# Slot sums over 32 features at a time, with VectorE's 32x32 turns in place of TensorE's transposes

## The chip, the cores and the metric

The kernel runs on one core of a Trainium2 chip. The metric is the device time of one execution in microseconds (us); three runs are given, and their median counts. One profiled execution gives the trace. Engines: PE is the matrix engine (PEld its weight loads), DVE is VectorE, ACT is ScalarE, POOL is GpSimd, SP issues most DMAs.

## What is computed

Attention with 32 memory slots for each of 8 batch entries and 8 heads (576 tokens, 64 features a head), then a mixture of 8 experts on the 4608 tokens. Cut to what matters:

```python
a = softmax(phi)                           # over 32 slots
k_m = einsum('bhsm,bhsd->bhmd', a, k)      # slot sums of the keys
v_m = einsum('bhsm,bhsd->bhmd', a, v)      # slot sums of the values
attn = softmax(q @ k_m.T / 8)
x = attn @ v_m                             # tokens x 512
e = argmax(normed(x) @ normed(emb).T / tau)
out = gate * relu(x @ w1[e]) @ w2[e]       # 512 -> 1024 -> 512
```

## The kernel before

The work goes batch by batch, `b` = 0 to 7, in a program order written out by hand; each engine runs its own list in that order. A batch has three parts on PE. `project(b)` (L610) multiplies the slot values by `w1` in two halves. `first(b)` (L629) is the expert's first layer, 16 steps of 6 matmuls. `second(b)` (L671, L682) is the second layer: 40 steps, 8 for the half tile and then 8 for each of four token tiles; a step of a full tile is three matmuls of 512 columns (`wh` and `hh`, `wl` and `hh`, `wh` and `hl`). `steps()` hangs the preparation of later batches on numbered steps: `first[n]` and `second[n]` hold calls that run after step n.

For batch `m = b + 2` the second layer of `b` carries: `softmax` (exponentials, ACT), `shares(m)` (reciprocals of the sums, `rs`), `turn` (PE transposes of the exponentials, copied by ACT into `eT`), and then the slot sums. There are six such batches, `b` = 0 to 5. `slots(m)` (L470) is 40 matmuls: for each of two groups `g` of four heads, four token chunks `kx` of 128 rows and a tail `kl` of 64 rows, one matmul a head with 32 slots as stationary columns and 128 moving columns (64 key, 64 value features). The four heads of a group fill four 32-column strips of the array, so four run side by side; with 64 rows eight do. All 40 stand in one visit, after step 31 (35 for `b` = 0). `blocks` (L504 on DVE, L506 on ACT) scales 32-row strips into `kvb`; `flip` (L514) turns `kvb` by four 128x128 transposes a group on PE, in two visits (steps 35 and 37; 38 and 39 for `b` = 0), and ACT copies the results into `kT` and `vT` (L517). `scores` (L530) and `squares` (L538) of the next batch read `kT` and `vT` right behind the next `project`.

Batches 0 and 1 are prepared before the loop, while DMA fills: `block` and `flip` for batch 0, then the first tokens' scores, whose expert choice `choose` lets SP fetch `w1` (L398). `flip(1, ...)`, `norm(0)` (L140) and `attend(1, 2)` (L115) stand between the two halves of `project(0)`; the second half writes the PSUM buffer that `norm(0)` reads.

A matmul of plain f32 stands as two records in the trace (two passes over the moving columns).

Of the kernel before, what the change touches and what calls it, by code (L numbers as in the profile page):

```python
# [8 lines left out]
F32 = mybir.dt.float32  # L9
# [3 lines left out]
AF = mybir.ActivationFunctionType  # L13
# [6 lines left out]
P = 128  # L20
# [211 lines left out]
class Kernel:  # L232
# [4 lines left out]
    def __init__(self, ctx, tc, phiT, qT, kv, kvt, emb, tau, w1, w2, out):  # L237
# [15 lines left out]
        self.kx = [st([P, H, 2 * D], F32, name=f"kx{k}") for k in range(4)]  # L253
        self.kl = st([P, 4, 2 * D], F32, name="kl")
        self.qt = st([P, NC, S], F32, name="qt")
        self.eT = st([P, 9, P], F32, name="eT")
        self.kvb = st([P, 2, NG, 4, D], F32, name="kvb")
        self.kb, self.vb = self.kvb[:, 0], self.kvb[:, 1]
        self.kT = st([P, NC, D], F32, name="kT")
# [33 lines left out]
    def consts(self):  # L293
        nc, st = self.nc, self.st.tile
        self.ident = st([P, P], F32, name="ident")
        make_identity(nc, self.ident)
        self.i8 = st([P, E], F32, name="i8")
        nc.gpsimd.iota(self.i8, pattern=[[1, E]], base=0, channel_multiplier=0, allow_small_or_imprecise_dtypes=True)
        self.rev8 = st([P, E], F32, name="rev8")
        nc.vector.tensor_scalar(out=self.rev8, in0=self.i8, scalar1=-1.0, scalar2=float(E), op0=ALU.mult, op1=ALU.add)  # L300

        self.eb = st([P, E], BF16, name="eb")
        nc.vector.tensor_scalar(out=self.eb, in0=self.i8, scalar1=1.0 / (E * P), scalar2=None, op0=ALU.mult)
        nc.vector.memset(self.vv, 0.0)

    def load_router(self):
        nc, st = self.nc, self.st.tile
# [62 lines left out]
    def load_kv(self, b):  # L370
        if b < B:
            for g in range(NG):
                to, x = self.kl[64 * g : 64 * g + 64], self.kvt[b, :, 4 * g : 4 * g + 4]
                (self.nc.sync if b else self.nc.scalar).dma_start(to, x)
            for k in range(4):
                self.nc.sync.dma_start(self.kx[k], self.kv[b, :, k])

    def load_q(self, b, halves=(0, 1)):
        if not b:
# [26 lines left out]

    def room(self, b):
        if b not in self.rs:
            self.rs[b] = [self.wk.tile([P, NG], F32, tag=t, name=f"{t}{b}") for t in ("nm", "sm", "rs")]
        return self.rs[b]  # L410

    def largest(self, b, g):
# [19 lines left out]
    def shares(self, b, gs=range(NG), v=None):  # L432

        v = v or self.nc.vector
        nm, sm, rs = self.room(b)
        for g in gs:
            for j in range(4) if g else (None,):
                src, dst = (slice(32 * x, 32 * x + 32) if g else slice(0, P) for x in (j, j ^ 1 if g else j))
                v.tensor_scalar(
                    out=rs[dst, g : g + 1], in0=sm[src, g : g + 1], scalar1=1e-9, scalar2=None, op0=ALU.add  # L440
                )
        g = slice(gs[0], gs[-1] + 1)
        self.nc.vector.reciprocal(out=rs[:, g], in_=rs[:, g])

    def turn(self, b, i0, i1):
        t = self.pt([P, 4, P], f"te{b}_{i0}")
# [5 lines left out]
        if i1 == 9 and b > 1:  # L452
            self.load_phi(b + 1)

    def slots(self, b, accs=None, gs=range(NG), ks=range(5), first=True, last=True):

        nc = self.nc
        if first:
            self.accs = accs or [self.pt([P, 2 * D], f"acc{b}_{g}") for g in range(NG)]
        accs = self.accs  # L460

        def to(i, g):
            r = slice(32 * i, 32 * i + 32)
            return accs[g][r, i] if len(accs[g].shape) == 3 else accs[g][r]

        def add(g, j, k):
            r = slice(64 * g, 64 * g + 64) if k == 4 else slice(P)
            e = self.eT[r, 4 * g + k if k < 4 else 8, 32 * j : 32 * j + 32]
            x = self.kl[r, j] if k == 4 else self.kx[k][:, 4 * g + j]
            nc.tensor.matmul(  # L470
                to(j ^ g, g), lhsT=e, rhs=x, start=first and k == ks[0], stop=last and k == ks[-1]
            )

        for g in gs:
            for k in ks:
                for j in range(4 if k < 4 else 0):
                    add(g, j, k)
        for j in range(4 if 4 in ks else 0):
            for g in gs:
                add(g, j, 4)  # L480
        if b > 1:
            self.load_kv(b + 1)

    def block(self, b, g, which=(0, 1), alone=False):

        nc = self.nc
        r = self.rs[b][2][:, g : g + 1]
        k, v = (x[:, g].rearrange("p (k i) d -> p k i d", i=2)[:, :, :: 1 - 2 * g] for x in (self.kb, self.vb))
        a = self.accs[g].rearrange("p (k i) d -> p k i d", i=2)
        if alone:  # L490
            nc.scalar.activation(k, a[..., :D], AF.Copy, scale=r)
        elif 0 in which:
            nc.vector.tensor_scalar(out=k, in0=a[..., :D], scalar1=r, scalar2=None, op0=ALU.mult)
        if 1 in which:
            nc.scalar.activation(v, a[..., D:], AF.Copy, scale=r)

    def blocks(self, b, g, vector=False):

        r, a = self.rs[b][2], self.accs[g].rearrange("p (s d) -> p s d", s=2)
        for j in range(4):  # L500
            n = slice(32 * (j ^ g), 32 * (j ^ g) + 32)
            to = self.kvb[n, :, g, j]
            if vector:
                self.nc.vector.tensor_scalar(out=to, in0=a[n], scalar1=r[n, g : g + 1], scalar2=None, op0=ALU.mult)  # L504
            else:
                self.nc.scalar.activation(to, a[n], AF.Copy, scale=r[n, g : g + 1])  # L506

    def flip(self, b, g, which=slice(2)):

        nc = self.nc  # L510
        for src, dst in ((self.kb, self.kT[:, 2 * g : 2 * g + 2]), (self.vb, self.vT[b % 2][:, g, :, :D]))[which]:
            t = self.pt([P, 3 * P], f"tf{b}_{g}{src is self.kb}")
            for k in range(2):
                nc.tensor.transpose(  # L514
                    t[:, k * P : k * P + P], src[:, g, 2 * k : 2 * k + 2].rearrange("p h d -> p (h d)"), self.ident
                )
            nc.scalar.copy(dst, t.rearrange("p (k m) -> p k m", k=2)[:, :, :D])  # L517

    def heads(self, gs=range(NG)):

# [6 lines left out]
    def score(self, b, ts, lo, hi):  # L527

        for g, j, r, c, i in self.heads():
            self.nc.tensor.matmul(ts[g][j], lhsT=self.kT[r, c, i], rhs=self.q(b, c)[r, lo:hi], start=True, stop=True)  # L530

    def squares(self, b, ts):

# [157 lines left out]
    def steps(self, b, t, u):  # L691
# [16 lines left out]
        if u:  # L708
# [30 lines left out]
            if m < B:  # L739
                for g in range(NG):  # L740
                    second[11 + 3 * g + o].append(lambda g=g: self.softmax(m, (g,)))
                second[18 + o].append(lambda: self.shares(m))
                second[(28 if b else 25) + o].append(lambda: [self.turn(m, i, min(i + 4, 9)) for i in (0, 4, 8)])
                at = second[(31 if b else 28) + o]
                at += [lambda: self.slots(m), lambda: self.blocks(m, 0), lambda: self.blocks(m, 1, True)]
                for g in range(NG):
                    second[(35 + 2 * g if b else 31 + g) + o].append(lambda g=g: self.flip(m, g))
        return first, second

    def batch(self, b, t, u):  # L750
# [8 lines left out]
        for k, _ in enumerate(self.project(b, self.vT[b % 2])):  # L759
            if not b:  # L760
# [147 lines left out]
def moe_linformer(ctx, tc, phiT, qT, kv, kvt, emb, tau, w1, w2, out):  # L908
# [8 lines left out]
    k.load_q(0)  # L917
    k.load_router()
    k.consts()
    accs = [k.ps.tile([P, 4, 2 * D], F32, tag=f"{n}3", name=f"acc0{n}", bufs=1) for n in "tm"]  # L920
    for acc in accs:
        k.nc.vector.memset(acc, 0.0)
    router = k.router()
    for g in range(NG):
        k.largest(0, g)
# [1 line left out]
    for i in (0, 4, 8):  # L927
# [2 lines left out]
            next(router)  # L930
        if i < 8:
            k.warm(2 if i else 4)
    k.shares(0)
    next(router)
    k.load_phi(1)
    t = Tokens(k, 0, k.pt)
    keys, values = slice(0, 1), slice(1, 2)
# [6 lines left out]
    k.flip(0, 0, keys)  # L944
    k.block(0, 1, which=(0,))
    k.flip(0, 1, keys)
# [4 lines left out]
    k.block(0, 1, which=(1,))  # L951
# [33 lines left out]
    for g in range(NG):  # L985
        k.part(g, slice(0, P), k.nc.scalar.copy)
    k.slots(1, accs)
    k.block(1, 0, alone=True)
    k.tags = 4
    k.block(1, 1, alone=True)  # L990
    t.divide(range(NG), others, True)
    t.turn(range(NG), others)
    k.load_w2(e)
# [37 lines left out]
```

## Time and profile before

| what | value |
|---|---|
| three runs | 417.06 us median (416.98 to 417.6) |
| profiled execution | 418.61 us, of which the span from first to last instruction is 416.8 us |
| PE | 404.8 us busy, 97% of the span |
| PEld, DVE | 329.2 us (79%), 261.9 us (63%) |
| ACT, POOL | 169.3 us (41%), 173.0 us (42%) |
| DMA | 91.16 MB, mean 219 GB/s |

The busy share is an average over the span; what one stage is worth is read from that stage's rows. Records of PE overlap, so the time that PE spends on something is read from the start of one record to the start of the next.

### The profile page before, as it was taken

The numbers are of one execution on the slowest core, as the hardware profiler recorded it, in microseconds if no ns is written. First come the engines' busy times: TensorE is split into PE (matmuls) and PEld (weight loads), VectorE is DVE, ScalarE is ACT, GpSimd is POOL, SyncE is SP. The second block draws the span as 40 slices with busy tenths as digits, with TensorE's granted clock in tenths as the row PEclk, the third lists the DMA queues.
The fourth block names the chain that finished last, engine by engine and source line by source line (L and its number), as shares of the span: only waits on it lengthen the run. The fifth ranks groups of instructions, "written<-read, shape, count | busy, mean of one in ns | idle before, by whom it ended". The sixth has DMA issues, their size and how long they took to land. (4 is left out here: it accounts for less than half of the span.)

```text
span 416.8 us, 9432 instructions
## 1 busy us (share of the span) xinstructions
PE 404.8 (97%) x3491; PEld 329.2 (79%) x3491; DVE 261.9 (63%) x839; ACT 169.3 (41%) x468; POOL 173.0 (42%) x205
## 2 busy tenths in 40 slices
PE   7879999999999999999999999999999999999995
PEld 3548878788887978879787888879788797869785
DVE  4697894679664795638773696647956386645100
ACT  4465522475225632357313752256323571045100
POOL 0035580387132941259130871329412591339100
PEclk9999999999999999999999999999999999999999
DMA  8999924896769924995459916699249504591011
GB/s 267 339 358 359 348 53 131 286 367 272 157 197 397 354 48 117 334 378 233 72 191 382 385 79 153 208 398 347 46 118 342 206 0 82 183 376 67 15 50 53
DMA packets 69856, 91.16 MB, mean 219 GB/s; under 512 B 41800, under 2 KB 47688, under 8 KB 69808
## 3 DMA queue, kind: packets, MB, share of 16 engines
q1 hardware_dynamic: 66928, 82.00, 59.5%
q0 software_dynamic: 2688, 8.26, 5.3%
q8 instruction: 28, 0.46, 0.5%
q10 hardware_dynamic: 192, 0.28, 0.3%
q14 instruction: 20, 0.16, 0.1%
HBM read 71.19 MB, written 19.33 MB: 217 GB/s over the span
## 5 line engine op out<-in xcount | busy, mean ns | idle before, releaser
L629 PE MATMUL ph<-aT,gh 128*128 128x288 f32 x512 | 103.3, 297 | 0.5 <-DVE gl L613 0.5
L682 PE MATMUL py<-wh,hh 128*128 128x512 f32 x248 | 102.4, 413 | 0.0
L682 PE MATMUL py<-wl,hh 128*128 128x512 f32 x248 | 97.1, 391 | 0.4 <-POOL wl L600 0.4
L682 PE MATMUL py<-wh,hl 128*128 128x512 f32 x248 | 97.2, 392 | 0.0
L600 POOL TENSOR_TENSOR wl<-w2s,wh 128x512 fp32r<-128x512 f32 x64 | 83.9, 1311 | 5.2
L629 PEld LDWEIGHTS ph<-aT,gh 128*128 128x128 f32 x512 | 81.7, 188 | 3.0 <-DVE gl L613 1.4
L629 PE MATMUL ph<-aT,gl 128*128 128x288 f32 x256 | 75.4, 295 | 0.0
L635 DVE SCALAR_TENSOR_TENSOR hl<-ph,hh 128x288 fp32r<-128x288 f32 x128 | 56.2, 450 | 21.1 <-ACT hh L632 15.7
L687 ACT ACTIVATE ys<-py,gate 128x512 f32<-128x512 f32 (+1 forms) x39 | 25.0, 641 | 103.8 <-PE py L682 55.0
L632 ACT ACTIVATE hh<-ph 128x288 fp32r<-128x288 f32 x128 | 52.2, 416 | 32.8 <-PE ph L629 32.0
L795 POOL DMA_DIRECT2D out_dram<-ys x28 | 15.5, 553 | 117.1 <-ACT ys L687 104.5
L682 PEld LDWEIGHTS py<-wh,hh 128*128 128x128 f32 x248 | 46.7, 188 | 12.0 <-issue 4.3
L682 PEld LDWEIGHTS py<-wh,hl 128*128 128x128 f32 x248 | 46.6, 188 | 10.2
L682 PEld LDWEIGHTS py<-wl,hh 128*128 128x128 f32 x248 | 46.8, 189 | 8.5 <-POOL wl L600 0.8
L629 PEld LDWEIGHTS ph<-aT,gl 128*128 128x128 f32 x256 | 48.1, 188 | 0.0
L590 POOL TENSOR_TENSOR aT<-aw,aT 128x576 fp32r<-128x576 f32 (+3 forms) x20 | 23.8, 1205 | 48.5 <-PE py L682 33.9
L599 POOL CAST wh<-w2s 128x512 fp32r<-128x512 f32 x64 | 42.4, 662 | 0.5 <-DMA w2s<-w 0.4
L613 DVE TENSOR_TENSOR gl<-pg,gh 128x512 fp32r<-128x512 f32 x32 | 20.0, 683 | 35.5 <-ACT gh L612 35.5
L671 PE MATMUL py<-w2s,h 128*64 128x256 f32 x256 | 29.4, 383 | 0.0
L120 DVE TENSOR_REDUCE lg<-po 128x8 f32<-128x16 f32 x40 | 6.9, 174 | 31.1 <-PE po L115 31.0
L671 PEld LDWEIGHTS py<-w2s,h 128*64 128x64 f32 x256 | 17.7, 137 | 9.4 <-DVE hl L635 1.0
L115 PEld LDWEIGHTS po<-vv,aw 128*128 128x128 f32 x160 | 21.8, 189 | 3.4 <-ACT kT L517 1.0
(168 smaller groups left out, 506.7 us busy)
## 6 DMA issues: line engine op xcount, KB each, us to landing
kx<-kv SPq DMA_DIRECT2D x32, 512.0 KB, 7.2
w2s<-w SPq DMA_DIRECT2D x32, 512.0 KB, 10.5
w1s<-w SPq DMA_DIRECT2D x28, 512.0 KB, 6.5
out_dram<-ys POOLq DMA_DIRECT2D x28, 256.0 KB, 6.0
qt<-qT SPq DMA_DIRECT2D x12, 576.0 KB, 8.3
ad<-aw SPq DMA_DIRECT2D x8, 576.0 KB, 13.1
td<-x SPq DMA_DIRECT2D x56, 72.0 KB, 2.2
ea<-td SPq DMA_DIRECT2D x7, 512.0 KB, 4.4
```

What stands on the lines that cost most here:

```text
L115: nc.tensor.matmul(po[:, 144 * g : 144 * g + P + E], lhsT=k.aw[:, g, to], rhs=k.vv[:, g], start=True, stop=True)
L590: self.nc.gpsimd.tensor_tensor(out=al, in0=a, in1=ah.bitcast(F32), op=ALU.subtract)
L599: (copy or self.nc.scalar.copy)(h, x)
L600: self.nc.gpsimd.tensor_tensor(out=l, in0=x, in1=h.bitcast(F32), op=ALU.subtract)
L613: nc.vector.tensor_tensor(out=self.gl[:, g, f], in0=ps[g], in1=self.gh[:, g, f].bitcast(F32), op=ALU.subtract)
L629: nc.tensor.matmul(p, lhsT=w[:, g, fs], rhs=x[:, g, to], start=g == 0 and k == 0, stop=g == 1 and k == 2)
L632: nc.scalar.activation(self.hh[:, f, to], p, AF.Relu)
L635: nc.vector.scalar_tensor_tensor(out=self.hl[:, f, to], in0=p, scalar=0.0, in1=self.hh[:, f, to].bitcast(F32), op0=ALU.max, op1=ALU.subtract)
L671: nc.tensor.matmul(p[64 * j : 64 * j + 64], lhsT=self.h4[:, f], rhs=self.w2s[:, f, d * j : d * j + d], start=f == 0, stop=f == 7,)
L682: nc.tensor.matmul(p, lhsT=h[:, f, to], rhs=w[:, f], start=f == 0 and k == 0, stop=f == 7 and k == 2)
L687: nc.scalar.activation(y[:, :d], p, AF.Copy, scale=gate[:, i : i + 1])
L795: eng.dma_start(self.out[r : r + P], y)
```

## The change

Each slot matmul becomes two of 64 columns: 32 key and 32 value features (`h` = 0, 1), which land in two strips. So a group's sums lie as rows (head of a pair, half of the features, slot) and columns (pair `c`, key or value, 32 features). One DVE multiplication a group (`scale`, L499 in the changed kernel) writes `ks`; one DVE turn in 32x32 blocks gives `kT`, four give `vT` (`keys`, `values`). PE's transposes, ACT's copies, `kvb` and the `blocks` scaling go. The sums are put in at five steps, one a token chunk. `shares` puts the reciprocals into four columns by eight small copies (POOL; DVE for batch 0). `vT` is cleared once at the start, and the clearing of `acc0t`, `acc0m` goes. The next batch's `load_kv` is issued behind the fifth visit.

```diff
 def shares
+        (v or self.nc.vector).tensor_scalar(out=sm, in0=sm, scalar1=1e-9, scalar2=None, op0=ALU.add)
+        self.nc.vector.reciprocal(out=sm, in_=sm)
+        for k in range(2):
+            for i in range(2):
+                src = slice(32 * (2 * k + i), 32 * (2 * k + i) + 32)
+                for h in range(2):
+                    dst = slice(64 * i + 32 * h, 64 * i + 32 * h + 32)
+                    (copy or self.nc.gpsimd.tensor_copy)(rs[dst, k::2], sm[src])
 def slots
+            for i in range(2):
+                j = 2 * c + i
...
+                for h in range(2):
+                    o = 64 * i + 32 * h
+                    nc.tensor.matmul(
+                        accs[g][o : o + 32, c],
+                        lhsT=e,
+                        rhs=x[:, :, 32 * h : 32 * h + 32],
...
+    def scale(self, b, g, which=slice(2), copy=False):
...
+            self.nc.vector.tensor_tensor(out=self.ks[:, 2 * g : 2 * g + 2, which], in0=x, in1=r, op=ALU.mult)
+    def keys(self, gs=range(NG)):
...
+        self.nc.vector.transpose(self.kT[:, c], self.ks[:, c, 0])
+    def values(self, b, gs=range(NG)):
+        for g in gs:
+            for i in range(2):
+                r, n = slice(64 * i, 64 * i + 64), 32 * (i ^ g)
+                self.nc.vector.transpose(self.vT[b % 2][r, g, :, n : n + 32], self.ks[r, 2 * g : 2 * g + 2, 1])
 def steps
-                at = second[(31 if b else 28) + o]
-                at += [lambda: self.slots(m), lambda: self.blocks(m, 0), lambda: self.blocks(m, 1, True)]
-                for g in range(NG):
-                    second[(35 + 2 * g if b else 31 + g) + o].append(lambda g=g: self.flip(m, g))
+                for n, k in zip((30, 32, 33, 35, 36) if b else (34, 35, 36, 37, 38), range(5)):
+                    second[n].append(lambda k=k: self.slots(m, ks=(k,), first=k == 0, last=k == 4))
+                second[n] += [lambda: self.scale(m, 0), lambda: self.scale(m, 1), self.keys, lambda: self.values(m)]
 def batch
-                    self.flip(1, 0)
-                    self.flip(1, 1)
+                    self.keys()
+                    self.values(1)
                     t.norm(0)
                     t.attend(1, 2)
 def moe_linformer (batch 0)
-    k.block(0, 0)
+    for g in range(NG):
+        k.scale(0, g, slice(0, 1))
+    k.keys()
+    for g in range(NG):
+        k.scale(0, g, slice(1, 2), copy=True)
...
-    k.flip(0, 0, values)
-    k.flip(0, 1, values)
     ts = [k.mm([P, S - P], f"tr0_{g}", g) for g in range(NG)]
     k.score(0, ts, P, S)
+    list(t.weigh(range(NG), first))
+    k.values(0)
     k.squares(0, [k.pt([P, D + E], f"tl0_{g}") for g in range(NG)])
-    list(t.weigh(range(NG), first))
```

PE in the second layer of a middle batch, before: `py` is the second layer's sum, `acc_0` and `acc_1` the slot sums of the two groups.

```order
L682 MATMUL py_2_1631<-wh,hl 128x512
L470 MATMUL acc_0_1702<-kx_70,eT 32x128 x4
L470 MATMUL acc_0_1702<-kx_71,eT 32x128 x4
L470 MATMUL acc_0_1702<-kx_72,eT 32x128 x4
L470 MATMUL acc_0_1702<-kx_73,eT 32x128 x4
L470 MATMUL acc_1_1703<-kx_70,eT 32x128 x4
L470 MATMUL acc_1_1703<-kx_71,eT 32x128 x4
L470 MATMUL acc_1_1703<-kx_72,eT 32x128 x4
L470 MATMUL acc_1_1703<-kx_73,eT 32x128 x4
L470 MATMUL acc_0_1702<-kl,eT 32x128
L470 MATMUL acc_1_1703<-kl,eT 32x128
```

The same place in the changed kernel, the last two of the five visits:

```order
L676 MATMUL py_3_1820<-wh,hl 128x512
L470 MATMUL acc_0_1792<-kx_73,eT 32x64 x8
L470 MATMUL acc_1_1793<-kx_73,eT 32x64 x8
L676 MATMUL py_3_1820<-wh,hh 128x512
L676 MATMUL py_3_1820<-wl,hh 128x512
L676 MATMUL py_3_1820<-wh,hl 128x512
L470 MATMUL acc_0_1792<-kl,eT 32x64 x4
L470 MATMUL acc_1_1793<-kl,eT 32x64 x4
L470 MATMUL acc_0_1792<-kl,eT 32x64 x4
L470 MATMUL acc_1_1793<-kl,eT 32x64 x4
L676 MATMUL py_3_1820<-wh,hh 128x512
```

One block of slot matmuls became five short ones with at least one step of the second layer between them; each count has doubled and each width halved.

DVE between the halves of batch 0's `project`, before:

```order
L613 TENSOR_TENSOR gl<-pg_00_494,gh 128x512
L613 TENSOR_TENSOR gl<-pg_01_495,gh 128x512
L140 ISA ea,ss_208<-po_0_347,ea 128x256
L140 ISA ss_208 128x1
L120 TENSOR_REDUCE lg_207<-po_1_529 128x8
```

and in the changed kernel:

```order
L607 TENSOR_TENSOR gl<-pg_00_573,gh 128x512
L607 TENSOR_TENSOR gl<-pg_01_574,gh 128x512
L504 STREAM_TRANSPOSE kT<-ks 128x128
L511 STREAM_TRANSPOSE vT_81<-ks 64x2x32 x4
L140 ISA ea,ss_212<-po_0_382,ea 128x256
L140 ISA ss_212 128x1
```

Batch 1's five turns now stand on DVE ahead of `norm(0)` (L140).

## Rows read from the trace of the kernel before

**Rows 1.** The page's first part: busy time, share of the span, instructions.
```profile
PE 404.8 (97%) x3491; PEld 329.2 (79%) x3491; DVE 261.9 (63%) x839; ACT 169.3 (41%) x468; POOL 173.0 (42%) x205
```
**Rows 2.** Waits of PE from 33 us on: us in total, times, longest.
```profile
PE ph L629 <- DVE gl L613: 0.5, 1, 0.5
PE py L682 <- POOL wl L600: 0.4, 1, 0.4
```
**Rows 3.** Timeline of PE, batch 1's second layer: start, us, instruction; around the slot sums.
```profile
122.68 0.39 PE L682 MATMUL py<-wh,hl 128*128 128x512 f32 x1
123.00 1.95 PE L470 MATMUL acc<-kx,eT 128*32 128x128 f32 x64
124.88 0.45 PE L470 MATMUL acc<-kl,eT 64*32 64x128 f32 x16
125.26 0.50 PE L682 MATMUL py<-wh,hh 128*128 128x512 f32 x1
125.60 0.40 PE L682 MATMUL py<-wl,hh 128*128 128x512 f32 x1
125.83 0.39 PE L682 MATMUL py<-wh,hl 128*128 128x512 f32 x1
```
**Rows 4.** The same timeline around the first group's transposes.
```profile
127.89 0.39 PE L682 MATMUL py<-wh,hl 128*128 128x512 f32 x1
...
128.47 0.48 PE L682 MATMUL py<-wh,hh 128*128 128x512 f32 x1
128.79 0.39 PE L682 MATMUL py<-wl,hh 128*128 128x512 f32 x1
```
**Rows 5.** The same timeline: scores and squares in 64x32 tiles, eight side by side.
```profile
134.09 0.70 PE L530 MATMUL tl<-qt,kT 64*32 64x288 f32 x16
134.58 0.34 PE L538 MATMUL tl<-vT 64*32 64x72 f32 x16
134.85 0.53 PE L629 MATMUL ph<-aT,gh 128*128 128x288 f32 x2
```
**Rows 6.** Groups of DVE and POOL by form: total us, mean ns, idle before.
```profile
L635 DVE SCALAR_TENSOR_TENSOR hl<-ph,hh 128x288 fp32r<-128x288 f32 x128 | 56.2, 450 | 21.1 <-ACT hh L632 15.7 <-ACT h L634 4.0
L613 DVE TENSOR_TENSOR gl<-pg,gh 128x512 fp32r<-128x512 f32 x32 | 20.0, 683 | 35.5 <-ACT gh L612 35.5
L93 DVE STREAM_TRANSPOSE aw<-x 128x64 f32<-128x64 f32 x16 | 3.2, 202 | 0.0
L439 POOL TENSOR_SCALAR rs<-sm 32x1 f32<-32x1 f32 x4 | 1.7, 422 | 0.3
```
**Rows 7.** Timelines of ACT (batch 1) and POOL (batch 0), a row each.
```profile
120.48 1.24 ACT L451 COPY eT<-te 128x512 f32<-128x512 f32 x3 [3.13 <-PE te L450]
...
72.89 2.90 POOL L590 TENSOR_TENSOR aT<-aw,aT 128x576 fp32r<-128x576 f32 x2 [5.92 <-DVE aT L589]
```
**Rows 8.** Timeline of the start, batch 0's first tokens, all engines.
```profile
13.15 0.48 DVE L493 TENSOR_SCALAR kvb<-acc0t,rs 128x256 f32<-128x256 f32 x1 [1.20 <-PE acc0t L470]
...
14.48 0.82 PE L530 MATMUL ts<-qt,kT 64*32 64x128 f32 x16
...
14.97 0.71 DVE L63 STREAM_TRANSPOSE x<-ts 128x128 f32<-128x128 f32 x2 [0.95 <-PE ts L530]
...
17.07 0.42 DVE L82 TENSOR_REDUCE z<-x 128x8 f32<-128x256 f32 x1 [0.48 <-ACT x L74]
```
**Rows 9.** The same timeline around the two halves of batch 0's project.
```profile
28.44 1.09 PE L610 MATMUL pg<-w1s,vT 64*32 64x512 f32 x16 [0.98 <-DMA w1s<-w]
...
30.18 1.29 DVE L613 TENSOR_TENSOR gl<-pg,gh 128x512 fp32r<-128x512 f32 x2 [0.76 <-ACT gh L612]
...
31.30 1.19 PE L115 MATMUL po<-vv,aw 128*128 128x136 f32 x8 [0.74 <-ACT kT L517]
31.39 0.41 DVE L140 CUSTOM_DVE_ANT_0 ea<-po,ea 128x256 f32<-128x256 f32 x1
...
32.86 1.09 PE L610 MATMUL pg<-w1s,vT 64*32 64x512 f32 x16
```

More of the change, by code (lines that the diff above doesn't have):

```diff
@@ L304, in consts @@
         nc.vector.memset(self.vv, 0.0)
+        for vT in self.vT:
+            nc.vector.memset(vT[..., :D], 0.0)
     def load_router(self):
@@ L408, in room @@
         if b not in self.rs:
-            self.rs[b] = [self.wk.tile([P, NG], F32, tag=t, name=f"{t}{b}") for t in ("nm", "sm", "rs")]
+            self.rs[b] = [self.wk.tile([P, n], F32, tag=t, name=f"{t}{b}") for t, n in (("nm", NG), ("sm", NG), ("rs", NC))]
         return self.rs[b]
@@ L430, in softmax, with shares @@
                 nc.gpsimd.tensor_copy(self.ex[:, S : S + 64], x[:, 4 * P :])
-    def shares(self, b, gs=range(NG), v=None):
-        v = v or self.nc.vector
+    def shares(self, b, v=None, copy=None):
         nm, sm, rs = self.room(b)
[L436 to L443, printed above, removed]
+        (v or self.nc.vector).tensor_scalar(out=sm, in0=sm, scalar1=1e-9, scalar2=None, op0=ALU.add)
[6 more added lines that the diff above has]
+                    (copy or self.nc.gpsimd.tensor_copy)(rs[dst, k::2], sm[src])
     def turn(self, b, i0, i1):
@@ L453, in turn, with slots, add @@
             self.load_phi(b + 1)
-    def slots(self, b, accs=None, gs=range(NG), ks=range(5), first=True, last=True):
+    def slots(self, b, accs=None, ks=range(5), first=True, last=True):
         nc = self.nc
         if first:
-            self.accs = accs or [self.pt([P, 2 * D], f"acc{b}_{g}") for g in range(NG)]
+            self.accs = accs or [self.pt([P, 2, 2, 32], f"acc{b}_{g}") for g in range(NG)]
         accs = self.accs
[L462 to L466, printed above, removed]
+        def add(g, k, c):
@@ L467, in add @@
             r = slice(64 * g, 64 * g + 64) if k == 4 else slice(P)
[L468 to L471, printed above, removed]
-            )
-        for g in gs:
[L475 to L517, printed above, removed]
+            for i in range(2):
+                j = 2 * c + i
+                e = self.eT[r, 4 * g + k if k < 4 else 8, 32 * j : 32 * j + 32]
+                x = self.kl[r, j] if k == 4 else self.kx[k][:, 4 * g + j]
+                for h in range(2):
[4 more added lines that the diff above has]
+                        rhs=x[:, :, 32 * h : 32 * h + 32],
+                        start=first and k == ks[0] and c == 0,
+                        stop=last and k == ks[-1] and c == 1,
+                        skip_group_check=True,
+                    )
@@ new lines, in slots @@
+        for g in range(NG):
+            for k in ks:
+                for c in range(2 if k < 4 else 0):
+                    add(g, k, c)
+        for c in range(2 if 4 in ks else 0):
+            for g in range(NG):
+                add(g, 4, c)
+        if b > 1 and last:
+            self.load_kv(b + 1)
+    def scale(self, b, g, which=slice(2), copy=False):
+        r = self.rs[b][2]
+        for c in range(2) if copy else ():
+            self.nc.scalar.activation(
+                self.ks[:, 2 * g + c, which], self.accs[g][:, c, which], AF.Copy, scale=r[:, 2 * g + c : 2 * g + c + 1]
+            )
+        if not copy:
+            x = self.accs[g][:, :, which]
+            r = r[:, 2 * g : 2 * g + 2].unsqueeze(2).unsqueeze(3).broadcast_to(x.shape)
+            self.nc.vector.tensor_tensor(out=self.ks[:, 2 * g : 2 * g + 2, which], in0=x, in1=r, op=ALU.mult)
@@ L529, in score @@
         for g, j, r, c, i in self.heads():
-            self.nc.tensor.matmul(ts[g][j], lhsT=self.kT[r, c, i], rhs=self.q(b, c)[r, lo:hi], start=True, stop=True)
+            self.nc.tensor.matmul(ts[g][j], lhsT=self.kT[r, c], rhs=self.q(b, c)[r, lo:hi], start=True, stop=True)
     def squares(self, b, ts):
@@ L919, in moe_linformer @@
     k.consts()
-    accs = [k.ps.tile([P, 4, 2 * D], F32, tag=f"{n}3", name=f"acc0{n}", bufs=1) for n in "tm"]
-    for acc in accs:
-        k.nc.vector.memset(acc, 0.0)
+    accs = [k.ps.tile([P, 2, 2, 32], F32, tag=f"{n}3", name=f"acc0{n}", bufs=1) for n in "tm"]
     router = k.router()
@@ L932, in moe_linformer @@
             k.warm(2 if i else 4)
-    k.shares(0)
+    k.shares(0, copy=k.nc.vector.tensor_copy)
     next(router)
@@ L941, in moe_linformer @@
             k.warm(2 if ks[0] == 2 else 1)
-    k.block(0, 0)
+    for g in range(NG):
+        k.scale(0, g, slice(0, 1))
+    k.keys()
+    for g in range(NG):
+        k.scale(0, g, slice(1, 2), copy=True)
     k.load_kv(1)
-    k.flip(0, 0, keys)
-    k.block(0, 1, which=(0,))
-    k.flip(0, 1, keys)
     first, others = slice(0, 4), slice(4, BL)
@@ L987, in moe_linformer @@
     k.slots(1, accs)
-    k.block(1, 0, alone=True)
     k.tags = 4
-    k.block(1, 1, alone=True)
+    for g in range(NG):
+        k.scale(1, g, copy=True)
     t.divide(range(NG), others, True)
```

16 lines of the change are left out of this document (7 added, 9 removed).

## The prediction

> **What bounds the kernel.** I read the page's busy shares first: PE is busy for 97% of the span, every other engine for 63% or less [rows 1]. A share alone proves nothing, so the waits of PE come next: from 33 us on it waits twice, for 0.9 us in all [rows 2]. From there to its last matmul PE's own list of work sets the time, and an edit is worth what it does to the distance between starts of PE's records. Only before 33 us do chains through DVE, ACT and DMA set it. So there are two sums: the steady part, six batches with slot sums in the second layer, and the start.
>
> **Steady part, before.** A second-layer matmul starts every 0.23 us (125.60 to 125.83). From 122.68 to 125.60, across the slot sums, there are 2.92 us where two spacings would take 0.46: the visit costs 2.46 us [rows 3]. A visit of the transposes, 127.89 to 128.79, costs 0.90 - 0.46 = 0.44 us, and there are two [rows 4]. Together 2.46 + 0.88 = 3.34 us a batch, and all of it is removed.
>
> **Steady part, after.** Streaming first. In 64x32 tiles, two passes over 288 columns start 0.49 us apart, so a column costs 0.245 / 288 = 0.85 ns a pass [rows 5]: 0.109 us for 128 columns, 0.054 for 64. Before, the 32 matmuls on `kx` are 64 records, four side by side, 16 passes x 0.109 = 1.74 of the 1.88 us from 123.00 to 124.88 [rows 3]. Now there are 32 passes of 0.054 on `kx` and 4 on `kl` (two before): 36 x 0.054 = 1.96 us, as before. Doubling the count and halving the width moves no streaming time.
>
> What grows is the number of visits. The same rows price the change between full 128x128 work and 32-column tiles: going in, 122.68 to 123.00 is 0.32 where 0.23 is usual, 0.09 more; coming out, 1.88 - 1.74 = 0.14 behind four-tile passes and 0.38 - 2 x 0.109 = 0.16 behind the eight-tile ones of `kl`; and the first matmul afterwards holds the next by 0.34 instead of 0.23, 0.11 more [rows 3]. The transposes, which keep the full array, show next to none of this: four of 128 columns at 0.109 are the whole 0.44 us [rows 4]. So a `kx` visit costs 0.09 + 0.14 + 0.11 + 8 x 0.054 = 0.77, four make 3.10; the `kl` visit 0.09 + 0.16 + 0.11 + 4 x 0.054 = 0.58. That is 3.68 us against 3.34: **+0.34 a batch, +2.0 us** over six.
>
> Unknown is the pace of a 128-row, 32-column pass when it is 64 columns wide; no row shows one. The nearest are the squares: two passes of 72 columns and the way out take 0.27 us, 134.58 to 134.85 [rows 5]; with 0.14 for the way out a pass is 0.065, at 64 columns about 0.06. I take 0.054, the price per column, which the pass of 128 columns keeps too, and hold 0.060 for the upper end (36 x 0.006 x 6 = +1.3 us). The changeover I keep at 0.03 either way (5 x 6 x 0.03 = 0.9 us), as its parts come from two-digit starts.
>
> The Trainium skill ("TensorE: Matmul & The Clock Gate", Part 3, The mechanism) says that a weight load runs beside a matmul in flight only if the row group differs. Here all `kx` tiles use all 128 rows, so by that rule each pass would show its loads; its section on LDWEIGHTS makes that about 27 ns for 32 columns (an estimate from the page). The row disagrees: 16 passes fit into 1.88 us with 0.14 left for the way out, so no load shows behind 128 columns [rows 3]. By the row the sum is the one below; what the rule would give stands with the rivals.
>
> **What covers the rest.** `eT`: ACT's copies end at 121.72 [rows 7], the first visit would start near 122.3, one step (0.69 us) before 123.00; 0.6 us of cover, and without it PE would wait once a batch for what is missing. DVE after the last visit: a multiplication of 128 columns is about 0.28 (683 ns at 512 columns and 450 at 288 give 1.04 ns a column [rows 6]), two of them; the key turn at most 0.36 [rows 8]; four value turns of 0.20 [rows 6]: keys after 0.9, all after 1.7 us. PE reaches the scores three steps (2.1) and a `project` later, whose halves take up to 1.09 each [rows 9]: about 4 us; in batch 0, with one step, about 2.6. Keys are in time; the gate operations and `gl` behind the value turns in batch 0 have under 1 us to spare, and what is late there would be `first`. POOL's eight copies, 0.42 at most each [rows 6], 3.4 us a batch, stand ahead of the two subtractions for `aT`, before which POOL idles 5.92 us [rows 7]. On SP, `load_kv` is issued some five steps (3.5 us) later at most, in the same place of SP's list and with the same bytes; it is needed a whole batch later: nothing. ACT loses its strip scaling and four copies a batch, for which PE did not wait [rows 2]: nothing gained.
>
> **The start.** Batch 0's first chain: scale at 13.15, transposes, copies, scores at 14.48, row turns at 14.97 [rows 8]. Now: two scales of 64 columns (0.22 each by the 1.04 ns), the second ready about 13.6, the key turn to 13.95, scores and 0.49 to the turns: 14.45, **0.5 earlier**. Then four value turns, 0.8, come between subtracting the maxima and the sums at 17.07, where DVE had waited 0.48 for the exponentials: 0.3 stays exposed, so 0.2 to 0.3 earlier at the expert choice. The fetch of `w1` follows the choice and PE waits 0.98 us for it [rows 9]; I pass on 0.3 (bounds 0 and 0.6: a busy DMA may keep all of it).
>
> Between the halves of `project(0)` PE loses eight transposes and the 0.74 us wait for ACT's copies ahead of 31.30 [rows 9]. But the second half waits for `norm(0)`, and batch 1's five turns now stand ahead of that on DVE: `gl` ends at 31.47 - 0.3, turns 1.16, norm 0.41, that is 32.7, or 32.2 if each starts a little before its predecessor ends, as norm did (31.39 against 31.47) [rows 9]. So the second half starts at about 32.4 instead of 32.86. **-0.5 us** in all, between +0.2 (nothing from the fetch, no overlap) and -1.0.
>
> **Sum.** +2.0 - 0.5 = +1.5 us. The profiled execution took 418.61, 1.55 above the median, and would become 420.1; on the median, 417.06 + 1.5 = **418.6 us**. Its own range: 2.0 - 0.9 - 1.0 = +0.1 to 2.0 + 0.9 + 1.3 + 0.2 = +4.4, 417.2 to 421.5. About 0.2% (0.83 us) is what a measurement can tell from no change.
>
> **Rivals.**
> *Faster: a short visit changes over more cheaply.* Place: the five entries and exits. If PE takes up the next tiles' loads while the array empties, because a visit is short, half the 0.34 to 0.36 would do: 5 x 0.17 + 1.96 = 2.8, -0.54 a batch, -3.2 - 0.5 = 413.4 us. It decides below 0.27 a visit. Against it: each change in the rows costs the same whatever follows, 0.09 in, 0.11 after. For it: only long visits are shown. 10%.
>
> *No change: the start gives more.* If the second half of `project(0)` followed its neighbours at once, PE would save the four pairs of transposes and the 0.74 wait, 1.8, and 0.3 from the fetch: +2.0 - 2.1, 417.0 us. Against it: the wait of that half on DVE. 13%.
>
> *Much slower: narrow passes don't halve.* If issue or loads hold all 36 passes at 0.109, each batch takes 36 x 0.055 = 1.96 more: +11.8, with the +1.5 430 us. For it: PE must start instructions twice as often as any row shows for 128-row tiles. Against it: two passes of eight 72-column tiles within 0.27 us [rows 5]. 6%.
>
> *Loads show.* With 64 columns to hide behind, a load that stays exposed for half a pass (0.027) makes 36 x 0.027 x 6 = +5.8, with the +1.5 424.4 us. Against it: behind 128 columns none shows. 5%. By the rule of the Trainium skill on row groups named above the new passes would behave like this.
>
> **Chances.** My forecast 66%: of it 52 slower by over 0.2%, 14 within. The two slow rivals add 11 to slower, the unchanged case 13 to within, the fast one 10 to faster: 0.10 faster, 0.27 same, 0.63 slower. The range 416.6 to 421.5 takes in the forecast and the unchanged case (79%) and leaves out the fast rival and the two slow ones.
>
> **What would show it.** Right: five 32-column visits a batch of about 0.77 and 0.58 us, starts of passes about 0.055 apart, entries 0.32 and exits with a first spacing of 0.34; no L514; no new wait of PE after 33 us; the first `project` at about 28.1 and its second half at about 32.4, waiting for DVE. Wrong: passes further apart than 0.06; a wait for `eT`, `kT` or `gl` in the steady part; a changeover under 0.27; or a second half of `project(0)` before 32.

## The result, and the profile after

The changed kernel takes **422.29 us** (median of 4 runs, 421.28 to 423.02), the kernel before 417.33 beside it (4 runs, 416.98 to 418.01): 1.0109 times as long, 95% interval 1.0092 to 1.0126. It is slower, as forecast, but by 5 us where 1.5 were forecast, and outside the range (421.5).

The page's first part of the changed kernel answers to [rows 1]: 576 more matmul records, nearly the same busy share, 17 us less ACT.

```profile
PE 407.7 (97%) x4067; PEld 325.1 (77%) x4067; DVE 261.8 (62%) x847; ACT 152.3 (36%) x414; POOL 181.9 (43%) x257
```

PE's waits from 33 us on answer to [rows 2]; columns as there. Only the first is new: the second half of batch 0's `project`, part of the start.

```profile
PE pg L604 <- DVE ss L140: 1.4, 1, 1.4
PE ph L623 <- DVE gl L607: 0.5, 1, 0.5
PE py L676 <- POOL wl L594: 0.3, 1, 0.3
```

PE's timeline in batch 1's second layer, the first visit and the last, answers to [rows 3]:

```profile
124.36 0.40 PE L676 MATMUL py<-wh,hl 128*128 128x512 f32 x1
124.69 0.65 PE L470 MATMUL acc<-kx,eT 128*32 128x64 f32 x32
125.27 0.50 PE L676 MATMUL py<-wh,hh 128*128 128x512 f32 x1
125.61 0.39 PE L676 MATMUL py<-wl,hh 128*128 128x512 f32 x1
...
131.68 0.40 PE L676 MATMUL py<-wh,hl 128*128 128x512 f32 x1
132.00 0.45 PE L470 MATMUL acc<-kl,eT 64*32 64x64 f32 x32
132.39 0.50 PE L676 MATMUL py<-wh,hh 128*128 128x512 f32 x1
132.72 0.39 PE L676 MATMUL py<-wl,hh 128*128 128x512 f32 x1
```

Read as in the prediction, a `kx` visit costs 1.25 - 0.46 = 0.79 us (0.77 forecast), the `kl` visit 1.04 - 0.46 = 0.58 (0.58 forecast).

To split the 5 us, the table takes starts of PE's first-layer matmuls from two traces of each kernel (the second ones were taken later, with the last experiments):

| | before | before, again | changed | changed, again |
|---|---|---|---|---|
| first layer of batch 0 starts at | 33.88 | 32.37 | 35.62 | 33.54 |
| from there to the end of PE's last matmul | 377.98 | 378.05 | 380.63 | 380.93 |
| from one middle batch to the next | 48.62 | 48.63 | 49.03 | 49.05 |

So **2.7 to 2.9 us are the steady part** (2.0 forecast). The start lost 1.2 us between the later traces and 1.7 between the earlier ones, **where 0.5 were to be won**; the medians, 4.96 apart, leave 2.1 to 2.3 for it, more than either pair of traces shows.

The start of the changed kernel, first trace, all engines:

```profile
14.92 0.96 PE L524 MATMUL tr<-qt,kT 64*32 64x448 f32 x8
...
17.49 1.22 PE L524 MATMUL tr<-qt,kT 64*32 64x448 f32 x4 [1.61 <-DMA qt<-qT]
...
17.88 0.46 PE L532 MATMUL tl<-vT 64*32 64x72 f32 x8
...
18.44 0.50 DVE L91 STREAM_TRANSPOSE aw<-x 128x128 f32<-128x128 f32 x2
...
19.57 0.91 ACT L570 COPY vv<-tl 64x72 f32<-64x72 f32 x4 [3.03 <-PE tl L532]
...
21.48 0.70 PE L115 MATMUL po<-vv,aw 128*128 128x136 f32 x4
```

DVE's chain ends with `aw` at 18.44, as before (18.43). But the choice needs `po`, `po` needs the squares `tl` through ACT's copies, and in PE's list the squares stand behind the scores of the remaining tokens, `tr`. `tr` is reached 1.2 us earlier than before, since the transposes are gone, and its second half stands still until the third part of q has landed. So `po` comes at 21.48 where it came at 18.89.

The windows of that stretch (last three columns: granted clock, DMA share, GB/s):

```profile
16.00:17.00 1.00, 0.00 (x0) 0.00 (x0) 0.91 (x5) 0.42 (x1) 0.00 (x0) 1.00 1.08 221
17.00:18.00 1.00, 0.51 (x9) 0.46 (x16) 0.87 (x5) 0.00 (x0) 0.00 (x0) 0.63 1.01 266
18.00:19.00 1.00, 1.00 (x18) 0.50 (x13) 0.96 (x4) 0.00 (x0) 0.00 (x0) 0.50 1.06 276
...
20.00:21.00 1.00, 1.00 (x4) 0.39 (x3) 0.00 (x0) 0.94 (x4) 0.00 (x0) 0.66 1.03 410
```

While PE waited, its clock was taken from 2.4 to 1.2 GHz, until 20.7 us, so that what followed ran at half speed. In the second trace PE waited even longer (1.88 us) at full clock (granted clock 1.00 from 14 to 20 us); its rows, behind those of the second trace of the kernel before:

```profile
15.34 0.98 PE L530 MATMUL tr<-qt,kT 64*32 64x448 f32 x16
...
16.12 0.33 PE L538 MATMUL tl<-vT 64*32 64x72 f32 x16
...
17.62 0.51 DVE L91 STREAM_TRANSPOSE aw<-x 128x128 f32<-128x128 f32 x2
...
18.08 0.70 PE L115 MATMUL po<-vv,aw 128*128 128x136 f32 x4 [0.44 <-DVE aw L91]
...
21.00 1.38 SPq L398 DMA_DIRECT2D w1s<-w  x2
```

```profile
13.93 0.96 PE L524 MATMUL tr<-qt,kT 64*32 64x448 f32 x8
...
16.77 0.91 PE L524 MATMUL tr<-qt,kT 64*32 64x448 f32 x5 [1.88 <-DVE z L83]
...
17.40 0.51 DVE L91 STREAM_TRANSPOSE aw<-x 128x128 f32<-128x128 f32 x2
...
19.40 0.70 PE L115 MATMUL po<-vv,aw 128*128 128x136 f32 x4
...
22.33 0.62 SPq L399 DMA_DIRECT2D w1s<-w  x1
```

(The row names DVE for the wait of 1.88; the semaphore that PE waits on there is the one of q's third transfer, whose last part landed at 16.63.) DVE is 0.22 us earlier, as forecast, and the choice 1.3 later.

Around batch 0's `project`, changed kernel, first trace, answering to [rows 9]:

```profile
29.85 1.09 PE L604 MATMUL pg<-w1s,vT 64*32 64x512 f32 x16 [0.88 <-DMA w1s<-w]
...
31.76 1.25 DVE L607 TENSOR_TENSOR gl<-pg,gh 128x512 fp32r<-128x512 f32 x2
...
33.15 0.96 DVE L511 STREAM_TRANSPOSE vT<-ks 64x64 f32<-64x64 f32 x4
...
34.12 0.42 DVE L140 CUSTOM_DVE_ANT_0 ea<-po,ea 128x256 f32<-128x256 f32 x1
...
34.60 1.09 PE L604 MATMUL pg<-w1s,vT 64*32 64x512 f32 x16 [1.44 <-DVE ss L140]
```

The second half starts 4.75 us after the first (4.42 before): `gl`, the turns and the norm one behind the other on DVE.

### The profile page after: what moved, and what is told of

Same layout as the page of the kernel before. It is cut to its first block, busy times and chain, and to the rows that moved or that the text cites. A ratio compares the mean times of both kernels' runs of the same rounds, so it can differ in the third digit from the quotient of the medians.

```text
span 421.2 us, 10573 instructions
## 1 busy us (share of the span) xinstructions
PE 407.7 (97%) x4067; PEld 325.1 (77%) x4067; DVE 261.8 (62%) x847; ACT 152.3 (36%) x414; POOL 181.9 (43%) x257
## 5 line engine op out<-in xcount | busy, mean ns | idle before, releaser
L676 PE MATMUL py<-wh,hh 128*128 128x512 f32 x248 | 104.1, 420 | 0.0
```

What stands on the lines that cost most here:

```text
L676: nc.tensor.matmul(p, lhsT=h[:, f, to], rhs=w[:, f], start=f == 0 and k == 0, stop=f == 7 and k == 2)
```

## The experiments

Medians stand beside runs of the kernel before on the same chip: 417.57 us (first four kernels), 417.71 (next four), 417.99 (the next two with a median), 417.39 (last two).

### The order at the start, and the norm

PE's scores of the remaining tokens go behind the squares and the copies of their products (lines left out are marked `...`):

```diff
-    k.score(0, ts, P, S)
...
     k.squares(0, [k.pt([P, D + E], f"tl0_{g}") for g in range(NG)])
     k.products(0)
...
+    k.score(0, ts, P, S)
```

> The changed kernel with one step moved: at the start PE's scores of the remaining tokens (tr) stand behind the squares and the copies of their products, so that the wait for the third part of q no longer stands ahead of the expert choice. If that wait and the half clock behind it made the start late (first layer of batch 0 at 35.6 instead of 33.9 us), the first po matmul comes back from 21.5 to about 18.9, the first project to about 28.4, and the time falls by about 1.4 us, to 420.9. If the fetch of w1 sets the start whatever the choice does, the choice comes earlier and the time falls by 0.3 or less, about 422.

422.79 us: a miss. The wait moved: the squares now waited 1.4 us for DVE's value turns, and the clock fell at 15.8 us all the same; `tr` still stood ahead of `po`, which came at 20.38.

On top of this, batch 1's turns go behind the norm:

```diff
-                    self.keys()
-                    self.values(1)
                     t.norm(0)
                     t.attend(1, 2)
+                    self.keys()
+                    self.values(1)
```

> The same, and batch 1's five turns on DVE stand behind norm(0) and attend(1, 2) instead of ahead of them. If the turns hold the second half of batch 0's project (the wait of 1.4 us for DVE), it starts some 1.1 us earlier, and the time is 1.1 below that of the kernel with the order alone, about 419.8. If something else releases that half (the attend matmuls, the copies of the first half), nothing more is won.

421.67 us by the median, 1.1 less, but its runs spread from 421.23 to 424.75, so the times alone don't show a gain, and the 419.8 that was expected was missed. The trace shows that the turns held the second half: it starts 3.89 us after the first, where 5.10 passed in the kernel with the order alone:

```profile
32.53 0.41 DVE L140 CUSTOM_DVE_ANT_0 ea<-po,ea 128x256 f32<-128x256 f32 x1
...
33.29 1.17 PE L604 MATMUL pg<-w1s,vT 64*32 64x512 f32 x16 [0.52 <-DMA w1s<-w]
```

### What a visit costs

```diff
-                for n, k in zip((30, 32, 33, 35, 36) if b else (34, 35, 36, 37, 38), range(5)):
+                for n, k in zip((31, 31, 31, 31, 31) if b else (35, 35, 35, 35, 35), range(5)):
```

> The changed kernel with all five token chunks of the slot sums in one visit, after step 31 (35 in batch 0); the same 64-column matmuls. If the price is one of changing the tile form, 0.33 us a visit, four visits less save 4 x 0.33 = 1.3 us a batch, six batches 8 us, 414.3. If the price lies in the narrow matmuls themselves, whichever visit they stand in, nothing changes: 422.3.

422.56 us by the median, where 414.3 were expected, but 419.24 to 424.75 by its runs. The profiled one, the fastest, shows part of the reason. In three middle batches the period is 47.75, 47.75 and 47.67 us: 1.3 less than with five visits, as the price says. In the next two it is 50.14 and 49.38. There PE stands still inside the slot sums, with no releaser:

```profile
266.80 1.75 PE L470 MATMUL acc<-kx,eT 128*32 128x64 f32 x107
270.64 0.53 PE L470 MATMUL acc<-kx,eT 128*32 128x64 f32 x21 [2.09 <-issue]
```

The kernel before with its own matmuls in five visits (batches 1 to 5); the two visits of the transposes move to steps 38 and 39 (not shown):

```diff
-                at = second[(31 if b else 28) + o]
-                at += [lambda: self.slots(m), lambda: self.blocks(m, 0), ...]
+                for n, k in zip((30, 31, 32, 33, 34) if b else (35,) * 5, range(5)):
+                    second[n].append(lambda k=k: self.slots(m, ks=(k,), first=k == 0, last=k == 4))
+                second[n] += [lambda: self.blocks(m, 0), lambda: self.blocks(m, 1, True)]
```

> The kernel before, with its 128-column slot matmuls in five visits at steps 30 to 34 in batches 1 to 5 (one visit as it was in batch 0), the scaling behind the last and the transposes at steps 38 and 39. If each visit costs about 0.33 us whatever the width, four more in five batches cost 4 x 5 x 0.33 = 6.6 us: 423.9. If a short visit of wide matmuls changes over for less, and the price belongs to the 64-column form, it stays within 2 us of the kernel before.

423.56 us, close to the 423.9 expected. A visit of four 128-column passes in its trace:

```profile
122.11 0.40 PE L682 MATMUL py<-wh,hl 128*128 128x512 f32 x1
122.44 0.64 PE L470 MATMUL acc<-kx,eT 128*32 128x128 f32 x16
123.01 0.50 PE L682 MATMUL py<-wh,hh 128*128 128x512 f32 x1
123.35 0.40 PE L682 MATMUL py<-wl,hh 128*128 128x512 f32 x1
```

1.24 - 0.46 = 0.78 us, the same as with eight narrow passes; the period is 49.82, 1.20 above the kernel before, 0.30 for each of four more visits. The price belongs to the visit, not to the width.

### The half clock

Six warm matmuls, which compute nothing that is used, fill PE's wait (the lines in `score` that call `half` between the two groups are left out):

```diff
-    k.score(0, ts, P, S)
+    k.score(0, ts, P, S, half=lambda: k.warm(6, 2))
```

> The changed kernel with one addition: six warm matmuls of PE (ones by ones, 1.3 us at full clock) between the scores of the first and of the second group of the remaining tokens, where PE waited 1.6 us for the third part of q. The output is the same. If the half clock from 17.4 to 20.8 us made the wait cost more than itself, the clock stays full, the way from the second group's scores to the first po falls from 3.99 to about 2.5 us, and the time falls by 1.4 us, to 420.9. If only the wait counts, or the fetch of w1 takes in what is won, it stays above 422.

423.1 us, where 420.9 were expected: the time didn't move, but the mechanism is there. The clock stayed at 2.4 GHz, and from the second group's scores to `po` it took 2.37 us instead of 3.99:

```profile
17.67 0.58 PE L526 MATMUL tr<-qt,kT 64*32 64x448 f32 x4
...
20.04 0.70 PE L115 MATMUL po<-vv,aw 128*128 128x136 f32 x4
```

Batch 0's first layer started at 34.25 instead of 35.62. In batch 1's `project` PE then stood still from 84.5 to 85.2 us, again with no releaser, and its first layer started at 88.14 where the first trace had 88.62: most of the gain was given back there.

### Fewer visits on a better start

With the warm matmuls and the norm ahead of the turns, two visits (`(30, 30, 30, 33, 33) if b else (34, 34, 34, 36, 36)`), three (`(30, 30, 32, 32, 35) if b else (34, 34, 36, 36, 37)`) and one:

> The changed kernel with the six warm matmuls, with batch 1's turns behind norm(0) and attend(1, 2), and with two visits instead of five: token chunks 0 to 2 after step 30, 3 and the tail after step 33 (34 and 36 in batch 0). By the price of a visit: 3 x 0.33 x 6 = 5.9 us less, 1.4 from the clock, 1.1 from the norm, 0.2 from the gates of batch 1: 413.7 us, faster than the kernel before. If PE's instructions come too slowly for long rows of narrow matmuls, as the gaps of 2.1 and 1.4 us with no releaser in the one-visit kernel suggest, there are such gaps here too and the time is 415 to 419.

> The same with three visits (chunks 0 and 1, 2 and 3, the tail). By the price of a visit 0.33 x 6 = 2 us more than with two, 415.7 us, a period of 48.6 - 0.3 = 48.35 us a batch; no gap without a releaser.

> The same with one visit. By the price of a visit alone 411.7 us. If instruction blocks come late in so dense a row, PE again stands still for 1 to 3 us inside the slot sums of some batches, with a 16 KB packet of the instruction queue under way at that time, in other batches than before since the program has moved, and the time lies between 413 and 419 with runs far apart.

| visits | median | range | period of an undisturbed middle batch |
|---|---|---|---|
| one | 419.45 | 415.74 to 424.03 | 47.72 |
| two | 417.18 | 415.47 to 418.55 | 48.09 |
| three | 419.06 | 418.04 to 421.21 | 48.30 |
| five (the change) | 422.29 | 421.28 to 423.02 | 49.03 |

(Medians and ranges of all runs; the one-visit kernel's median without its three longest, 421.99 to 424.03, is 418.05. The five visits stand on the old start here.) The periods follow the price: (49.03 - 47.72) / 4 = 0.33 us a visit. The medians of two and three are 3.4 to 3.5 us above what was expected: in both traces batch 1's `project` and scores took 3.9 to 4.0 us up to the first layer where before they took 3.0, and in the last batch, where `w1` came late, they took 3.8 and 3.5 instead of 2.5.

The first visit of the two-visit kernel has 24 passes:

```profile
122.19 1.55 PE L470 MATMUL acc<-kx,eT 128*32 128x64 f32 x96
123.67 0.50 PE L678 MATMUL py<-wh,hh 128*128 128x512 f32 x1
```

They take 1.48 us to the next full matmul, where eight take 0.58 (124.69 to 125.27): 0.90 / 16 = 0.056 us a pass, and 0.58 - 8 x 0.056 = 0.13 for the way out.

Two visits are a little faster than the kernel before (0.9983, interval 0.9969 to 0.9997). One visit has stops again:

```profile
266.29 1.65 PE L470 MATMUL acc<-kx,eT 128*32 128x64 f32 x101
270.91 0.64 PE L470 MATMUL acc<-kx,eT 128*32 128x64 f32 x27 [2.98 <-issue]
```

The stops cost more than their own length: behind this one and the next the granted clock is 0.50 (1.2 GHz) for 3.4 us each, from 271.7 and from 322.9, and the two batches take 52.58 and 51.89 us, 4.9 and 4.2 above the undisturbed ones, where the stops alone are 2.98 and 2.44.

Counted over PE's and PEld's records in order of start, these two kernels go on after their stops at records 5825 and 6849, in both of them, though one has 12 records more at the start; the stop of the warm kernel in batch 1 ends at record 1985, as does one of 1.13 us there in the second one-visit kernel. All are 193 above a multiple of 256. The slot sums stop in the same batches as in the first one-visit kernel, then, and not in others, as was expected. A packet of the instruction queue is under way in each of the four stops in the slot sums; in the DMA view of this kernel from 268.2 to 269.6 us:

```profile
q8 instruction: 1, 0.02, 4.3%
```

It holds 16,384 bytes, 64 for each of 256 instructions. In the first one-visit kernel PE passed record 5569 at 262.94, the next packet started 5.5 us later, at 268.44, took 0.94, and PE went on 1.26 us after its end. In this kernel the same packet starts 7.1 us behind that record. The test moves the program against these blocks:

```diff
-    k.warm(11)
+    k.warm(4)
+    for _ in range(48):
+        hot = k.mm([P, 512], "hot", 0)
+        k.nc.tensor.matmul(hot[:, :8], lhsT=k.ones, rhs=k.ones[:, :8], start=True, stop=True)
```

> The one-visit kernel with its long gaps, but 48 tiny warm matmuls at the start in place of seven long ones, which moves the rest of PE's program by 82 records of the trace. If PE stops where a block of 256 instructions ends (the three stops so far are at records 1985, 5825 and 6849, all 193 more than a multiple of 256), the boundaries now come 30 to 140 records into the 320 of each visit, so that the next block is used up at the visit's end, within 2 to 5 us: stops of 0.5 to 4 us behind or late in the visits of most of the six batches, still at records 193 more than a multiple of 256, and a time of 420 to 430. If the stops come from the work itself (data, a buffer), they stay in the slot sums of batches 4 and 5 and move by 82 records, and the time is that of the one-visit kernel.

437.0 us. The 48 matmuls alone took 10.4 us (2.97 to 13.39), where the seven that they replace took 0.43 each; I had not foreseen that, and the time lies above what was expected. The stops moved: one of 4.6 us in the start, then

```profile
92.27 0.34 PE L470 MATMUL acc<-kl,eT 64*32 64x64 f32 x14
95.24 0.38 PE L470 MATMUL acc<-kl,eT 64*32 64x64 f32 x18 [2.63 <-issue]
...
141.09 0.40 PE L678 MATMUL py<-wl,hh 128*128 128x512 f32 x1
144.71 0.50 PE L678 MATMUL py<-wh,hl 128*128 128x512 f32 x1 [3.23 <-issue]
```

and one of 1.4 in the batch after: three of the six batches, where most were expected. The batches that stopped before run at 47.72. The stops end at records 961, 1985, 3009 and 4033, all 193 above a multiple of 256 again. So the stops follow the blocks of PE's instructions, and not the work of a batch.

### The start mended

The two-visit kernel with `tr` behind the choice:

```diff
-    ts = [k.mm([P, S - P], f"tr0_{g}", g) for g in range(NG)]
-    k.score(0, ts, P, S)
+    k.warm(8)
...
     e = t.choose((0,))
+    ts = [k.mm([P, S - P], f"tr0_{g}", g) for g in range(NG)]
+    k.score(0, ts, P, S)
...
-            k.warm(7, hot=t.spare)
+            k.warm(1, hot=t.spare)
```

> The two-visit kernel with the scores of the remaining tokens (tr) behind the expert choice instead of ahead of the squares; in their old place stand eight warm matmuls, and six of the seven behind the choice go. If q's third part and the half clock behind the wait made the choice late, the first po comes at about 18.9 (20.0 in the two-visit kernel), w1 is asked for 1.1 us earlier and batch 0's first layer starts at 31.9 to 32.2 instead of 33.3: 1.1 to 1.4 us less than the two-visit kernel, about 415.9. If batch 1's project takes it back, as it did with the warm matmuls alone, the time stays at 416.7 to 417.2.

**415.14 us**, 0.9927 times the kernel before (0.9905 to 0.9949), the fastest of all: 2.0 us below the kernel with `tr` in its old place, a little more than expected. Not all of that is the start: the first layer, at 32.65, came later than expected. Of the 2.1 us between the spans of the two traces 0.65 lie ahead of it, 0.24 in batch 0, and 1.25 in the last batch, where `w1` came late in the one and not in the other. PE in its trace:

```profile
16.73 0.32 PE L532 MATMUL tl<-vT 64*32 64x72 f32 x4
...
19.07 0.70 PE L115 MATMUL po<-vv,aw 128*128 128x136 f32 x4
...
20.52 0.98 PE L524 MATMUL tr<-qt,kT 64*32 64x448 f32 x16
...
27.35 1.09 PE L604 MATMUL pg<-w1s,vT 64*32 64x512 f32 x16 [0.32 <-DMA w1s<-w]
```

The second traces of both kernels:

> The kernel before once more, for a second trace of its start. The first profile waited 6.5 us from the issue of w1 to its landing, where the kernel with five old visits, the same until then, waited 5.3. If that was chance, batch 0's first layer starts at about 32.6 here instead of 33.9.

> The changed kernel once more, for a second trace of its start. If the wait for q and the half clock belong to the change and not to one execution, PE waits over 1 us between the two groups' scores again, and batch 0's first layer starts 2 us or more later than in the second trace of the kernel before.

They took 417.19 and 421.27 us, and batch 0's first layer starts at 32.37 and 33.54, as in the table above. The wait for q is there again, 1.88 us; the half clock isn't. The 2 us between the starts were not reached: 1.2.

Last, the edits of the start on the five-visit kernel, `tr` alone, then also the norm ahead of the turns:

> The changed kernel with its five visits, and one edit at the start: the scores of the remaining tokens behind the expert choice, eight warm matmuls in their old place, six warm matmuls less behind the choice. If their place in PE's list, ahead of the squares, is the step that made the start late, batch 0's first layer starts at about 33.1 us instead of 33.5 (without the half clock) or 35.6 (with it), and the median falls by 1 to 2 us, to 420.3 to 421.3. If the two-visit kernel won its 2 us only because it had two visits, nothing changes: 422.3.

> The same, and batch 1's turns behind norm(0) and attend(1, 2). The start is then the one of the fastest kernel (first layer at 32.65), within 0.3 us of the kernel before, and what stays of the difference is the steady part with five visits: 0.41 us a batch, six batches, and 0.2 to 0.3 behind batch 0, 2.7 us: 417.7 + 2.7 = 420.4. If the start's loss has another cause, it stays above 421.5.

421.02 us (420.25 to 422.22) and 420.30 (419.12 to 420.76). By the medians the place of `tr` is worth 422.29 - 421.02 = 1.3 us and the place of the turns 0.7; each of the two is at the edge of the noise, both together, 2.0, are clear of it (1.0092 to 1.0126 against 1.0046 to 1.0077 of the kernel before). The rest, 420.30 - 417.39 = 2.9 us, is the steady part (2.7 to 2.9 in the traces).

The first of the two traces shows the choice mended, but not the start. `po` came at 18.00 and `w1` was asked for at 20.93 us, 1.4 earlier than in the second trace of the changed kernel, yet the first layer came at 33.75 (33.1 expected). Fifteen of the 16 parts of the first `w1` transfer had landed by 26.44, 5.5 us after the request; the last one came at 27.97. In the second of the two traces, with the last part 0.9 behind the others, the first layer starts at 32.82.

## Why the prediction was wrong

**What bounds the kernel.** Right: from 33 us on PE's own list sets the time, and no wait came but the one that was named.

**The steady part** was right in its mechanism and 0.07 us a batch short. 3 x 0.79 + 0.77 + 0.58 = 3.72 us against 3.34 is +0.38, the periods say +0.41, forecast was +0.34. The terms of the visit held nearly one by one: a narrow pass takes 0.056 us (0.054 forecast), the way out of a `kx` visit 0.13 (0.14), the way in 0.33 - 0.23 = 0.10 (0.09), the first matmul afterwards 0.11 more (0.11).

**What covers the rest.** Right for `eT`, the keys and POOL. For batch 0 I named the cover that was thin, under 1 us for the gate operations and `gl`, and then charged nothing. In batch 1's `project` `gl` starts 2.47 us after PE (87.91 against 85.44) where it was 1.74 before (85.01 against 83.27). From the first layer of batch 0 to that of batch 1 the changed kernel takes 53.00 us, before 52.36: 0.23 more than the visits explain. In the second traces it is 0.37 more; there PE's loads also paused 0.61 us inside that `project`, with no releaser, at record 1985.

**The start is the step that failed**: "0.2 to 0.3 earlier at the expert choice", and with it "-0.5 us". I followed DVE's chain, and there it held (`aw` 17.40 against 17.62). But the choice needs PE too, and PE runs its list in order: `tr`, which waits for q, stands ahead of the squares. Before, the transposes filled the time until q had landed; the forecast took them out and never asked when it lands. Here it landed later, too. My bounds (+0.2 to -1.0) had no case in which the choice gets later. It came 1.3 us later in the trace at full clock and 2.6 in the one with the half clock; undoing both gave 2.0 us (1.3 for the place of `tr`, 0.7 for that of the turns). Of the 3.5 us by which the difference of the medians was missed, 2.6 to 2.8 belong to the start and 0.7 to 0.9 to the steady part. That the time came out less than 1 us beyond the range is luck: the room kept there for slower passes and changeovers wasn't needed for them, and covered most of what the start lost.

The second half of `project(0)` was named with its reason, but 4.3 us behind the first half; it is 4.75 in both traces. `gl`, turns and norm follow each other without the overlap that I took from one pair of rows.

**The rivals.** "Faster: a short visit changes over more cheaply" fell: a visit costs 0.33 on the average of five against one (single steps 0.21 to 0.37), and 0.30 with wide passes. "Narrow passes don't halve" and "Loads show" fell with the pass of 0.056. The Trainium skill ("TensorE: Matmul & The Clock Gate", Part 3, The mechanism) has weight loads run beside a matmul only where the row group differs. The trace disagrees for these tiles: all 128 rows in each, and no load shows behind 64 columns: a pass takes 0.056 us for 64 and 0.109 for 128. "No change: the start gives more" looked at the place that mattered, with the wrong sign.

**What stays open.** Why q's third transfer lands later in the changed kernel. It lands in 16 parts; in both traces of the changed kernel 15 of them are there by 16.01 and 14.95 us, about when PE comes, and the last at 17.36 and 16.63, where before the last is within 0.2 to 0.3 us of the others (three traces). A 16 KB instruction packet is under way just before (14.60 and 13.55); but in some of the other kernels with the new start the last part isn't late, and no run moved the packet alone. Open too is why a wait of 1.61 us lowered the clock and one of 1.88 didn't, and why an instruction packet starts 5.5 and 7.1 us after PE has passed a block's end, at 268.44 in both traces. How often `w1` of the last batch comes late in the kernels with two and three visits, one trace of each doesn't tell.

## What to carry to other kernels

When work is taken out ahead of an instruction that waits for a transfer, ask first when that transfer lands, and then what stands behind the instruction in its engine's list: what another chain needs should stand ahead of it. Price short visits of another tile form by the visit, not by the columns, and put them together as long as the row of short instructions stays under a block of instructions (visits of 192 and 128 records had no stop here, those of 320 had). And a forecast that names a thin cover should also charge for it.

## What the runs showed of the hardware

PE can run out of instructions. At some 120 records a us (107 matmul records and as many loads in the 1.75 us of the one-visit row), a visit of 320 records can reach the end of a block before the next is there. It did in two of six batches in both one-visit kernels, and in three with the program moved: stops of 1.4 to 3.2 us, all ending at records 193 above a multiple of 256. Five visits of 64 records each had none in the second layer, nor had two or three visits. The Trainium skill ("Runtime: NRT & Kernel Launch", Instruction fetch mechanics) gives blocks of 16 KiB, 256 instructions, fetched while the block before runs, and says that the crossing is mostly hidden. The runs agree on the size of the blocks. That the crossing is hidden holds here for most blocks, but not for the stops above.

Changing between full tiles and 32-column tiles costs PE about 0.3 us a visit (0.30 with wide passes; 0.37, 0.21 and 0.37 from one to two, two to three and three to five narrow visits), and the passes in between stream at 0.85 to 0.88 ns a column (0.109 us for 128, 0.056 for 64).

What waits for a transfer waits for the last of its 16 parts. PE went on at 17.49 and 16.77 us, 0.13 and 0.14 behind the last part of q's third transfer and 1.5 and 1.8 behind the 15th. That last part came 0.8 us or more behind the 15th in eight of the thirteen traces of kernels with the new start.
